# Half the sines of the even phases, wider evacuations, reordered cross sums, and two product differences made by negation and accumulating DMAs

## The chip, the cores and the metric

The kernel runs on one core of a Trainium2 chip, as one launch. The metric is the device time of the launch in microseconds (us), lower is better. The core has five engines that run side by side and wait for one another by semaphores: TensorE (PE, matmuls, with PEld for its weight loads), VectorE (DVE), ScalarE (ACT), GpSimd (POOL) and SyncE (SP, which only issues DMAs here). POOL issues the accumulating DMAs, which add a tile in SBUF to another one.

## The reference

Two branches over a sequence of 2048 positions and 640 channels, mixed by a gate for each position:

```python
def _A_ref(q, k, v, shift_k, ssm_k, ssm_D):
    k_shift = sum over t of k_pad[:, t:t + S, :] * shift_k[:, ks - 1 - t]   # ks = 4
    kv = k_shift * v
    y_f = rfft(kv padded to 2S) * rfft(ssm_k padded to 2S)                  # along the sequence
    y = irfft(y_f)[:S].astype(bfloat16)
    y = y + kv * ssm_D
    return q * y

def _B_ref(x, w1, b1, w2, b2):
    h = layernorm(x)                                    # over the 640 channels
    u = gelu(einsum("bsd,sf->bdf", h, w1) + b1)         # F = 1536
    y = einsum("bdf,fs->bds", u, w2) + b2
    return y.transpose(0, 2, 1)

g = sigmoid((q * gate_w).sum(-1, keepdims=True))
out = g * _A_ref(q, ...) + (1 - g) * _B_ref(q, ...)
```

The first branch is a long causal convolution for each channel, the second an MLP over the sequence dimension.

## The kernel before

The MLP is two streams of 384 matmuls of 128x128 by 128x320: `m1` (`pp<-X,ring`, weights from w1, followed by a gelu on ScalarE) and `m2` (`pp<-GT,W`, weights from w2). The convolution is done as a transform by matrices of sines (`FTB`, [128, phase 4, kt 2, cos/sin 2, k2 2, 128]), with the sequence split into four phases p and two halves h. The filter's transform (`wT` to `C[0]`, `C[1]`) and the signal's (`kv` to `C[2]`, `C[3]`) are matmuls on TensorE, evacuated from PSUM by ScalarE, and then mixed by VectorE with additions of 128x2560 (`mixing`, `mixing_acc`). Pointwise complex products follow (`cross`, `product`), then the inverse mixing (`invmix`) and the inverse transform (`inverse`, `pp<-C,FTB` and `pp<-SS,FTB`), whose evacuations are scaled by the gate, multiplied by q and added to the MLP's result `O1`.

What sets the order. The kernel doesn't write its instructions in the order of the code. Each operation is handed to a list planner (`_Sched`) with a duration, a priority and its dependencies. `run` plays the engines forward and picks, for each, the ready operation of lowest priority number; `emit` then writes the instructions in that order, and a tracker adds the semaphore waits. So the order on each engine is fixed at build time by the planner's own durations, and on the chip an engine waits in that order whatever else is ready. `after` edges force an order without a wait. In `run` a DMA gets an end: for every queue the transfer follows the DMAs before it at 365 GB/s, plus 2 us, and plus 6 us more if POOL issues it.

What the change and the prediction's steps touch:

- The head. `zz` spins (`SPIN`, line 798, and `WSPIN`, line 980) are matmuls on zeros put ahead of the filter's transposes and of the first transform. For each phase VectorE computes integer angles (`pint`), ScalarE takes a sine of 1024 elements. `transp` (line 862) transposes the filter through TensorE, `fwd_c` (line 878) transforms it in 16 groups of 4 matmuls of 320 columns, each evacuated by one ACTIVATE of 128x640.
- `k_turn` (line 760): a VectorE copy `kp<-kn` and a DMA transpose `KT<-kp` on SP. The first two turns stand between the layer norm statistics and their application. The third and fourth copies wait for two further k loads, which stand on SP behind the first two transposes.
- `kv` (line 1066): the short convolution, `pp<-KF,KT`, which needs both transposes of its half; its product `vkv<-ksh,vkv` or `kv<-ksh,v` is on VectorE.
- `mixing_acc` (line 1104): for each of two slots i, VectorE writes R(i) - R(2+i) to another place, and then a POOL DMA adds R(2+i) to R(i). Sums that read R(0) and R(1), written `C<-C`, wait for both DMAs.
- `product` (line 1201) with `into`: one product goes by an accumulating DMA into another tile, the real part is a 5120-wide product into `tm` and a subtraction.
- `acc_dma` (line 1222): two accumulating DMAs that add one of the products to another; they feed the second `invmix`.
- `inverse` (line 1275): TensorE needs the outputs of `invmix` from VectorE, phase by phase.
- W (w2) is loaded by SP, in pieces that wait until TensorE has finished with the part of `ring` that they overwrite.

The W loads and the accumulating DMAs share the core's DMA engines.

Of the kernel before, what the change touches and what calls it, by code (L numbers as in the profile page):

```python
# [9 lines left out]
BF16 = mybir.dt.bfloat16  # L10
# [3 lines left out]
ACT = mybir.ActivationFunctionType  # L14
# [314 lines left out]
class _Sched:  # L329
# [59 lines left out]
    def run(self):  # L389
# [14 lines left out]
        port = {"DVE": 0.0, "POOL": 0.0}  # L404
        dma_free = 0.3
        avail = {}
        for op in ops:
# [7 lines left out]
        t = 0.0  # L415
# [4 lines left out]
        while started < n:  # L420
# [6 lines left out]
            for e in engs:  # L427
# [31 lines left out]
                if e in ("SP", "QA") or op.lat < 0:  # L459
                    issue = 1.2 if e == "POOL" else 0.1  # L460
                    s = max(t + issue, dma_free)
                    dma_free = s + op.dur
                    op.end = dma_free + 2.0 + (6.0 if e == "POOL" else 0.0)
                    free[e] = t + issue
                else:
                    op.end = t + op.dur
                    if op.lock:
                        op.end += max(port["POOL" if e == "DVE" else "DVE"] - t, 0.0)
                        port[e] = op.end
                    free[e] = op.end  # L470
# [44 lines left out]
def _build(nc, A_q, A_k, A_v, A_shift_k, A_ssm_k, A_ssm_D, B_x, B_w1, B_b1, B_w2, B_b2, gate_w, out):  # L515
# [10 lines left out]
    with ExitStack() as es:  # L526
# [27 lines left out]
        def base_of(h):  # L554
            return T.mem[h.name][1]
# [56 lines left out]
        q_hi = alloc("q_hi", [128, 2, 4, D], BF16, at=base_of(Drow))  # L612
        assert base_of(KF) == base_of(Drow) + 1280
        cgb = [alloc(f"cgb{i}", [128, 2, D], BF16, at=base_of(GTB) + 2560 * i) for i in range(3)]

# [181 lines left out]
        memset("DVE", zz[:, :], 0.0, prio=-1)  # L797
        SPIN = (7, 3, 3, 2, 2)

# [9 lines left out]
        iota(acol[:, :], [[0, 1]], 0, 8)  # L809
        jr = lambda p, kt: iota(jrow[:, 2 * p + kt, :], [[-512 * (4 * kt + p), 2], [4 * (4 * kt + p), 128]], 4096 + 4 * kt + p, 0)  # L810
        for p in PORD:
            for kt in range(2):
                jr(p, kt).dur = 0.34
            if p == PORD[0]:
                iota(dif[:, :], [[1, 128]], 0, -1)
        iota(dif2[:, :], [[1, 32]], 128, -1)
# [6 lines left out]
        sins = {}  # L823
        for p in PORD:
            pv = V(pint, 1024 * p, [[512, 2], [256, 2], [1, 256]])
            t_ = tt("DVE", pv, V(tb, 0, [[0, 2], [256, 2], [1, 256]]), V(jrow, 512 * p, [[256, 2], [0, 2], [1, 256]]), ALU.add)
            if p != 0:
                t_.after.add(pprev)
            pa = pint[:, p, :, :, :].rearrange("q a b c -> q (a b c)")
            pprev = ts("DVE", pa, pa, 4095, None, ALU.bitwise_and, mode=4)  # L830
            if p == 0:
                ts("DVE", ident[:, :], dif[:, :], 0.0, None, ALU.is_equal)
            sins[p] = act(FTB[:, p, :, :, :, :].rearrange("q a b c d -> q (a b c d)"), pa, ACT.Sin, bias=cst[:, 0:1],
                scale=-(2.0 * math.pi / 4096.0) * (1.0 - 1e-6), name="sin")
        SC.add("DVE", 0.6, lambda s: T.op("DVE", lambda e: e.tensor_copy(ro, ri), [ri], [ro]), [ri], [ro], prio=0, name="taps")
# [26 lines left out]
        def transp(h, db):  # L862
            vt = _VT("cv")
            items = []
            for kt in range(2):
                for p in range(4):
                    o = (lambda s, j=4 * kt + p: s[:, 128 * j:128 * j + 128])
                    dfold = h == 0 and kt == 0 and p == 0
                    if dfold:
                        items.append((o, ident[0:1, :], Drow[0:1, 128 * db:128 * db + 128], True, False))  # L870
                    items.append((o, V(ssm, db * S + 1024 * h + 4 * kt + p, [[8, 128]]), ident[:, :], not dfold, True))
            m_ = mms(vt, (spin(SPIN[db]) if h == 0 else []) + items, name="wtr")
            m_.dur = (0.65 + 0.31 * SPIN[db] if h == 0 else 0.55)
            o_ = act(V(wT, 2 * h * SL + 128 * db, [[SL, 2], [D, 4], [1, 128]]), (lambda s: s[:, :].rearrange("q (a b c) -> q a b c", a=2, b=4)), ACT.Copy, vt=vt, name="wT")
            if h == 0:
                o_.after.add(sins[0 if db == 0 else 2])

        def fwd_c(p, ci, dst, scale):
            for k2 in range(2):
                vt = _VT("cv")  # L880
                items = []
                for kt in range(2):
                    for c in range(2):
                        items.append((chk(c), FTB[:, p, kt, c, k2, :], srcW(0)(kt, p, ci), kt == 0, kt == 1))
                m_ = mms(vt, (spin(WSPIN) if (p, ci, k2) == (PORD[0], 0, 0) else []) + items, name="W")
                m_.dur = 0.54
                act(V(dst, p * SL + k2 * D + 320 * ci, [[2 * D, 2], [1, 320]]), two, ACT.Copy, vt=vt, name="We", scale=scale)

# [59 lines left out]
        def ln_tile(hk, p):  # L948
# [6 lines left out]
            if t == 0:  # L955
                ops[0].after.add(pprev)
            o, i = mv[:, t, :], stats[:, t, :]
            ops.append(SC.add("DVE", 0.12, (lambda o, i: lambda s: T.op("DVE", lambda e: e.bn_aggr(o, i), [i], [o]))(o, i), [i], [o]))
# [20 lines left out]
        KFP = (0, 5, 10, 15)  # L979
        WSPIN = 3  # L980
        srcW = lambda h: (lambda kt, p, ci: wT[:, 2 * h + kt, p, 320 * ci:320 * ci + 320])
        for h in range(2):
            for db in range(ND):
                transp(h, db)
            if h == 0:
                consts()
            if h in (1,):
                fwd_even(srcW(h), h, C[h], 1.0 / 1024.0, h == 1, "W")
# [6 lines left out]
            if h == 0:  # L995
# [11 lines left out]

                pag = []

                def flush():  # L1010
# [5 lines left out]
                def stats_of(k):  # L1016
                    for t in range(LB[k], LB[k + 1]):
# [5 lines left out]
                        seq.append(b1)  # L1023
                        pag.append(ag)
                    ln_scale(LB[k], LB[k + 1])
                stats_of(0)
# [9 lines left out]
                for hk in range(2):  # L1036
                    k_turn(hk)
                mixing(C[0], SS, 0, fine=True, prio=MIXP)
            else:
# [161 lines left out]
        def product(dst, a, v, late=None, into=None):  # L1201
            if into is not None:
                tt("DVE", late, H(a, 1), H(v, 0), ALU.mult)
                dma(H(into, 1), late, 128 * 5120, stream="POOL", prio=0, accum=True)
                tt("DVE", P2(T0), P2(a), P2(v), ALU.mult)
                tt("DVE", H(dst, 1), H(a, 0), H(v, 1), ALU.mult)
                tt("DVE", H(dst, 0), H(T0, 0), H(T0, 1), ALU.subtract)
                return
# [116 lines left out]
        chained(product, A1[1], A1[1], V0[1], tmp_of(q_hi, 0), V1[1])  # L1325
        chained(product, A1[0], A1[0], V0[0], tmp_of(q_hi, 1), V1[0])
        acc_dma(A1[1], V1[1])
        acc_dma(A1[0], V1[0])
        chained(product, A0[1], A0[1], V0[1], H(V0[1], 0))
        lastacc = SC.ops[-1]  # L1330
        assert lastacc.eng == "POOL"
        for kt in range(2):
# [46 lines left out]
```

## Time and profile before

| | us |
|---|---|
| median of 3 runs | 180.29 (179.93 to 180.88) |
| the profiled execution | 179.5 |
| its span, first to last instruction | 177.7 |
| TensorE busy | 172.6 |
| VectorE busy | 169.7 |
| ScalarE busy | 117.0 |

The granted TensorE clock is 1.000 over the whole span. The difference between the profiled execution's time and its span, 1.8 us, lies outside the program's instructions. In the page each digit of a slice stands for a tenth of 4.4 us; a line of the order of time gives the start, the busy time, engine, source line, operation and tiles (buffer numbers left out), and in brackets an idle time before it and what ended it. For a DMA the trace also has the time from issue to landing. All matmuls have line L298 and all two-operand VectorE operations L632, so they are told apart by their tiles.

### The profile page before, as it was taken

The numbers are of one execution on the slowest core, as the hardware profiler recorded it, in microseconds if no ns is written. First come the engines' busy times: TensorE is split into PE (matmuls) and PEld (weight loads), VectorE is DVE, ScalarE is ACT, GpSimd is POOL, SyncE is SP. The second block draws the span as 40 slices with busy tenths as digits, with TensorE's granted clock in tenths as the row PEclk, the third lists the DMA queues.
The fourth block names the chain that finished last, engine by engine and source line by source line (L and its number), as shares of the span: only waits on it lengthen the run. The fifth ranks groups of instructions, "written<-read, shape, count | busy, mean of one in ns | idle before, by whom it ended". The sixth has DMA issues, their size and how long they took to land.

```text
span 177.7 us, 3342 instructions
## 1 busy us (share of the span) xinstructions
PE 172.6 (97%) x1380; PEld 129.4 (73%) x1381; DVE 169.7 (96%) x203; ACT 117.0 (66%) x176; POOL 43.6 (25%) x52
## 2 busy tenths in 40 slices
PE   7999999799999999999999999999999999999993
PEld 2666787487788776777777778888888887777772
DVE  7899789989999999999999999999999999999974
ACT  4999997998999999529999911231321323754760
POOL 8089803300000065000241101204343000252000
PEclk9999999999999999999999999999999999999999
DMA  4999999999999999999999998898999999499363
GB/s 136 394 411 374 391 312 156 248 414 374 191 240 315 109 216 226 231 228 278 230 227 271 205 248 299 144 225 230 188 193 217 207 218 408 167 197 212 93 241 131
DMA packets 38542, 43.51 MB, mean 245 GB/s; under 512 B 15867, under 2 KB 31360, under 8 KB 38528
## 3 DMA queue, kind: packets, MB, share of 16 engines
q1 hardware_dynamic: 33296, 32.16, 61.2%
q0 software_dynamic: 5200, 11.14, 36.5%
q8 instruction: 11, 0.18, 0.5%
q14 instruction: 3, 0.02, 0.0%
q10 hardware_dynamic: 32, 0.01, 0.0%
HBM read 25.87 MB, written 2.62 MB: 160 GB/s over the span
## 4 chain that ended last, share of the span: by engine, by line
PE 88%; DMA 5%; ACT 3%; SPq 2%; issue 0%; DVE 0%
PE pp L298 88%; DMA rows<-in_B_b_dram 5%; SPq L272 2%; ACT C L676 1%; ACT L676 1%; ACT GT L676 0%; DVE O L688 0%
## 5 line engine op out<-in xcount | busy, mean ns | idle before, releaser
L298 PE MATMUL pp<-X,ring 128*128 128x320 bf16 x384 | 55.3, 299 | 0.0
L632 DVE TENSOR_TENSOR C<-C 128x2560 bf16<-128x2560 bf16 (+2 forms) x37 | 54.5, 1523 | 0.8 <-ACT C L676 0.6
L298 PE MATMUL pp<-GT,W 128*128 128x320 bf16 x384 | 52.6, 299 | 0.0
L298 PEld LDWEIGHTS pp<-GT,W 128*128 128x128 bf16 x384 | 43.5, 113 | 8.7
L298 PEld LDWEIGHTS pp<-X,ring 128*128 128x128 bf16 x384 | 37.3, 98 | 14.3
L676 ACT ACTIVATE C<-pp 128x640 bf16<-128x640 f32 x64 | 40.7, 731 | 2.8 <-PE pp L298 2.7
L676 ACT ACTIVATE O<-pp,c,omg 128x640 bf16<-128x640 f32 x15 | 13.3, 885 | 34.7 <-PE pp L298 34.7
L267 POOL DMA_DIRECT2D C<-C x8 | 11.0, 1616 | 43.9 <-DVE C L632 43.9
L298 PE MATMUL pp<-wT,FTB 128*128 128x320 bf16 x112 | 17.1, 299 | 0.7 <-ACT GT L676 0.5
L676 ACT ACTIVATE cgb<-pp,gg 128x640 bf16<-128x640 f32 x16 | 12.7, 795 | 5.6 <-PE pp L298 5.2
L676 ACT ACTIVATE GT<-pp,cc 128x640 bf16<-128x640 f32 x12 | 9.6, 803 | 9.3 <-PE pp L298 9.2
L298 PEld LDWEIGHTS pp<-wT,FTB 128*128 128x128 bf16 x112 | 10.5, 98 | 5.6 <-ACT GT L676 0.8
L632 DVE TENSOR_TENSOR tm<-C,C 128x2560 bf16<-128x2560 bf16 (+1 forms) x7 | 14.3, 2059 | 0.0
L954 DVE BATCH_NORM_STATS2 stats<-X 128x6 f32<-128x320 bf16 x32 | 13.6, 464 | 0.5 <-DMA X<-in_A_q_dram 0.5
L298 PE MATMUL pp<-C,FTB 128*128 128x320 bf16 x96 | 13.4, 299 | 0.0
L267 POOL DMA_DIRECT2D C<-q_hi x6 | 5.9, 977 | 27.6 <-DVE C L632 12.9
L298 PEld LDWEIGHTS pp<-C,FTB 128*128 128x128 bf16 x96 | 9.4, 98 | 3.6
L676 ACT ACTIVATE gq<-gq 128x640 bf16<-128x640 bf16 x16 | 11.8, 745 | 0.2 <-DVE gq L632 0.2
L632 DVE TENSOR_TENSOR SS<-C 128x2560 bf16<-128x2560 bf16 x8 | 11.7, 1488 | 0.1
L632 DVE TENSOR_TENSOR C<-tm 128x2560 bf16<-128x2560 bf16 (+1 forms) x9 | 10.7, 1194 | 0.1
L676 ACT ACTIVATE ksh<-pp 128x1024 bf16<-128x1024 f32 (+1 forms) x12 | 9.9, 903 | 0.2 <-PE pp L298 0.2
L267 POOL DMA_DIRECT2D O<-q_hi x4 | 4.8, 1200 | 21.3 <-DVE q_hi L632 21.3
(77 smaller groups left out, 197.0 us busy)
## 6 DMA issues: line engine op xcount, KB each, us to landing
ring<-in_B_w_dram SPq DMA_DIRECT2D x12, 512.0 KB, 12.2
W<-in_B_w_dram SPq DMA_DIRECT2D x12, 512.0 KB, 5.5
C<-C POOLq DMA_DIRECT2D x8, 640.0 KB, 11.5
X<-in_A_q_dram SPq DMA_DIRECT2D x4, 640.0 KB, 8.4
kn<-in_A_k_dram SPq DMA_DIRECT2D x4, 640.0 KB, 9.4
out_dram<-O SPq DMA_DIRECT2D x7, 320.0 KB, 3.4
C<-SS POOLq DMA_DIRECT2D x3, 640.0 KB, 11.9
ssm<-in_A_ssm_k_dram SPq DMA_DIRECT2D x3, 512.0 KB, 6.8
```

The costliest lines, as they stand in the source:

```text
L267: ins = engobj.dma_start(out_ap, in_ap, accum_op=ALU.add, max_dma_last_dim=2560)
L272: ins = engobj.dma_start(out_ap, in_ap)
L298: ins = self.nc.tensor.matmul(ps_ap, lhsT=lhsT, rhs=rhs, start=start, stop=stop, skip_group_check=True)
L632: o_ = SC.add(eng, d, lambda s: T.op(eng, lambda e: e.tensor_tensor(o, a, b, op), rd, [o]), rd, [o], prio=prio, name="tt")
L676: return T.op("ACT", lambda e: e.activation(o, src, func, **kw), rr + [src], ww)
L954: ops.append(SC.add("DVE", 0.38, (lambda o, i: lambda s: T.op("DVE", lambda e: e.bn_stats(o, i), [i], [o]))(o, i), [i], [o]))
```

## The change

1. Sines. One ScalarE sine gives half of phases 0 and 2 (four blocks of 128 for each); phases 1 and 3 are as before. The other half of phases 0 and 2 is written by four VectorE multiplications with +1 or -1 out of the first half. The iotas that make the angles are cut to match.
2. Spins: 7, 1, 1, 1, 1 instead of 7, 3, 3, 2, 2, and none instead of 3 before the first transform.
3. Evacuations in `fwd_c`: 8 groups of 384 columns by two (768 evacuated at once), and 4 groups of 256 by four (1024 at once).
4. A small gelu right after the second half's transposes, which brings the table load with it.
5. The first two `k_turn` copies are put behind the statistics of tiles 13 and 15.
6. The planner's model of POOL DMAs: they follow each other at 2.2 times their transfer time, 1.8 us after issue at the earliest, beside the other queues.
7. `product` with `into`: the 5120-wide product and the subtraction become two products of 2560; the one to be subtracted is negated by ScalarE and added by an accumulating DMA.
8. The four DMAs of the two `acc_dma` calls are put behind the accumulate of the third product.

By items 6 and 7 the planner also moves operations that are not in the diff. On VectorE the two subtractions of `mixing_acc` for the last transform now stand together, and the two `C<-C` sums that read its DMAs stand eight product steps and the gate's sum after them, ahead of most of the products of `cross`. On TensorE the first inverse transform stands after 296 matmuls of `m2` (320 before), with 8 and 40 between and after its parts (40 before), and 40 at the end (24 before).

```diff
+        acc_free = 0.0
...
-                    s = max(t + issue, dma_free)
-                    dma_free = s + op.dur
-                    op.end = dma_free + 2.0 + (6.0 if e == "POOL" else 0.0)
+                    if e == "POOL":
+                        acc_free = max(t + issue + 0.6, acc_free) + 2.2 * op.dur
+                        op.end = acc_free
+                    else:
+                        s = max(t + issue, dma_free)
+                        dma_free = s + op.dur
+                        op.end = dma_free + 2.0
...
-        SPIN = (7, 3, 3, 2, 2)
+        SPIN = (7, 1, 1, 1, 1)
...
+            so = V(FTB, 0, [[2048, 2], [256, 4], [1, 128]]) if n_ == 0 else V(FTB, 1024 * (1, 3)[n_ - 1], [[1, 1024]])
+            si = V(pint, 0, [[512, 2], [128, 4], [1, 128]]) if n_ == 0 else pa
+            sins[(0, 1, 3)[n_]] = act(so, si, ACT.Sin, bias=cst[:, 0:1], scale=-(2.0 * math.pi / 4096.0) * (1.0 - 1e-6), name="sin")
+        for o_, i_, sg in (((640, 256), (512, 256), -1.0), ((128, 256), (0, 256), 1.0), ((2432, 256), (2048, 768), -1.0), ((2176, 768), (2304, 256), 1.0)):
+            h_ = ts("DVE", V(FTB, o_[0], [[o_[1], 2], [1, 128]]), V(FTB, i_[0], [[i_[1], 2], [1, 128]]), sg, None, ALU.mult, mode=4)
...
         def fwd_c(p, ci, dst, scale):
+            if ci == 1:
+                vt = _VT("cv")
+                items = []
+                for k2 in range(2):
+                    for c in range(2):
+                        for kt in range(2):
+                            items.append(((lambda s, j=2 * c + k2: s[:, 256 * j:256 * j + 256]), FTB[:, p, kt, c, k2, :], wT[:, kt, p, 384:640], kt == 0, kt == 1))
+                m_ = mms(vt, items, name="W")
+                act(V(dst, p * SL + 384, [[D, 4], [1, 256]]), lambda s: s[:, :].rearrange("p (a f) -> p a f", a=4), ACT.Copy, vt=vt, name="We", scale=scale)
+                return
...
-        WSPIN = 3
+        WSPIN = 0
...
+                g_ = act(gws[:, :], cst[:, 1:2], ACT.Gelu_apprx_tanh, name="tab", prio=SC.ops[-1].idx)
+                g_.after.add(SC.ops[-2])
...
                     k_turn(hk)
+                    SC.ops[-2].after.add(kpos[hk])
...
             if into is not None:
                 tt("DVE", late, H(a, 1), H(v, 0), ALU.mult)
                 dma(H(into, 1), late, 128 * 5120, stream="POOL", prio=0, accum=True)
-                tt("DVE", P2(T0), P2(a), P2(v), ALU.mult)
+                tn = (V(ngb, 0, [[1280, 2], [1, 1280]]), H(T1, 1))[npr[0]]
+                npr[0] += 1
+                tt("DVE", tn, H(a, 1), H(v, 1), ALU.mult)
+                act(tn, tn, ACT.Copy, scale=-1.0, prio=0, name="neg")
+                dma(H(into, 0), tn, 128 * 5120, stream="POOL", prio=0, accum=True)
                 tt("DVE", H(dst, 1), H(a, 0), H(v, 1), ALU.mult)
-                tt("DVE", H(dst, 0), H(T0, 0), H(T0, 1), ALU.subtract)
+                tt("DVE", H(dst, 0), H(a, 0), H(v, 0), ALU.mult)
                 return
...
+        n_acc = len(SC.ops)
         acc_dma(A1[1], V1[1])
         acc_dma(A1[0], V1[0])
         chained(product, A0[1], A0[1], V0[1], H(V0[1], 0))
         lastacc = SC.ops[-1]
+        for o_ in SC.ops[n_acc:]:
+            if o_.eng == "POOL" and o_ is not lastacc:
+                o_.after.add(lastacc)
```

## The prediction

> **What bounds the kernel now.** I read the page's busy sums and slices first, then the chain of work that ended last, then TensorE and VectorE in order of time, then the landing of single DMAs.
>
> The page's busy sums and slices, and two pieces of the chain:
>
> ```profile
> PE 172.6 (97%) x1380; PEld 129.4 (73%) x1381; DVE 169.7 (96%) x203; ACT 117.0 (66%) x176; POOL 43.6 (25%) x52
> ...
> PE   7999999799999999999999999999999999999993
> ...
> DVE  7899789989999999999999999999999999999974
> ...
> DMA  4999999999999999999999998898999999499363
> ```
>
> ```profile
> 35.02 139.97 PE pp L298 x1128
> 174.99 0.03 issue
> 175.02 0.55 DVE O L688
> ```
>
> TensorE runs without a gap from 35.02 to 174.99 us: it is the bound. But VectorE is at 96% too, and the DMA engines are full in nearly every slice. TensorE stays fed only because the second MLP product (`m2`, 384 matmuls) can be put before the inverse transforms, which need VectorE's results. So I look at where the two meet, in VectorE's and TensorE's order of time:
>
> ```profile
> 140.87 8.50 DVE L632 TENSOR_TENSOR C<-C 128x2560 bf16<-128x2560 bf16 x6
> ```
>
> ```profile
> 148.73 8.86 PE L298 MATMUL pp<-C,FTB 128*128 128x320 bf16 x64
> ```
>
> The fifth of these six sums is the first input of the inverse; at 1.42 us each it ends at 140.87 + 7.1 = 147.97. TensorE arrives at 148.73. VectorE is ahead by 0.76 us only, after 320 `m2` matmuls.
>
> Two places upstream fix when VectorE gets there. First, the copy that waits for the third k load, and an early wait for ScalarE (VectorE in order of time):
>
> ```profile
> 36.10 3.63 DVE L632 TENSOR_TENSOR C<-C 128x1280 bf16<-128x1280 bf16 x3 [0.65 <-ACT C L676]
> 39.94 0.83 DVE L764 COPY kp<-kn 128x2560 bf16<-128x2560 bf16 x1 [0.21 <-DMA kn<-in_A_k_dram]
> ```
>
> Second, the accumulating DMAs of `mixing_acc`, issued by POOL, and the sums that read their result:
>
> ```profile
> L267 POOL DMA_DIRECT2D C<-C x1: 1200/1200/1200, 84.9 to 84.9; - x1
> ...
> DMA to landing us min/median/max: 7.2/7.2/7.2
> ```
>
> ```profile
> L267 POOL DMA_DIRECT2D C<-C x1: 1200/1200/1200, 88.8 to 88.8; - x1
> ...
> DMA to landing us min/median/max: 10.7/10.7/10.7
> ```
>
> ```profile
> L272 SPq DMA_DIRECT2D W<-in_B_w_dram x3: 368/385/814, 85.9 to 88.1; - x3
> ...
> DMA to landing us min/median/max: 7.2/7.9/10.9
> ```
>
> ```profile
> 83.11 1.49 DVE L632 TENSOR_TENSOR C<-C 128x2560 bf16<-128x2560 bf16 x1
> ...
> 86.79 1.49 DVE L632 TENSOR_TENSOR C<-C 128x2560 bf16<-128x2560 bf16 x1
> ...
> 101.19 2.89 DVE L632 TENSOR_TENSOR C<-C 128x2560 bf16<-128x2560 bf16 x2
> ```
>
> The producers run at 83.11 and 86.79; the DMAs land at 84.9 + 7.2 = 92.1 and 88.83 + 10.7 = 99.6, because four W loads share the engines; the consumer comes at 101.19, 1.6 us after. The reader should see that this margin is small and that VectorE shows no gap there.
>
> **What the Trainium skill says.** "DMA: Bandwidth & Descriptors", section "Issuing engines are not separate DMA queues": DMAs of SP and POOL run on the same 16 engines and interleave. The trace agrees: an accumulate of 640 KB takes 5.8 us to land at 122.2, in quieter traffic, and 10.7 beside the W loads. "TensorE: Matmul & The Clock Gate", section "What's actually happening": TensorE's clock halves after an idle window of some 3.4 us. The trace fits at the start only: seven warm-up matmuls of 512 columns take 3.17 us, three later ones 0.81. "ScalarE activation tables: per-element evaluation and per-set limits", section "What a function is on this engine", puts two functions of different sets one table load, 1283 ns, apart; the trace has 1.28 us.
>
> **The change, part by part.**
>
> Head (half sines, wider evacuations, fewer spins, table load). One of four sines goes (1.06 us from start to start on ScalarE). Twelve evacuations replace sixteen: 640 columns cost 0.585 us apart and 1024 cost 0.905 (rows at 13 to 27 us), so 768 is worked out at 0.692; 8 x 0.692 + 4 x 0.905 = 9.16 against 9.36. Four small VectorE products (some 0.15 each, estimated from the 128x256 row at 0.30 in a slower mode) replace a pair of 0.69 + 0.42; both sit before X lands, where VectorE idles 0.5, so nothing. Nine of twenty spin matmuls go: 9 x 0.21 = 1.9 us of TensorE, but they only filled waits. The table load (1.28) moves from 31.60, before the first gelu that TensorE waits for, into ScalarE's 0.88 us idle at 27.8. Before 35.02 TensorE shows 1.2 us of waits behind these. TensorE then reaches the conv product `kv` 1 to 2 us earlier, where KT lands at 33.9 as now (the moved k turn costs nothing: the first still starts at about 22.7, when kn lands, and the second transpose is issued at 27.95 behind the first). After the second KT landing (51.1) I keep a gain of 1.25 us for TensorE; bounds 0 and 2.2.
>
> VectorE gains 1.3 to 2 us up to 37.7, and loses it all: the copy of the third k tile waits for kn at 39.9, and that load is queued on SP behind the two transposes, which do not move. From there to the 80s the changed order holds the same VectorE operations, so it is where it was: gain 0.
>
> Products. Each of the two on A1 loses one 5120-wide product (2.87) and two or three 2560-wide steps change places: 14.63 us for both from 110.40 to 125.03 becomes 4 x 1.45 x 2 = 11.6, so VectorE saves 3.0. ScalarE gets two negations of 2560 (0.72 for the 640-wide bf16 row, and 1920 more elements at the 0.32 us that lie between 640 and 1024: 2.3 us each), in idle gaps of 2.4 between O evacuations. POOL gets two more 640 KB accumulates.
>
> Reordering. TensorE's order now has 296 `m2` matmuls before the inverse instead of 320, so it wants its first input 24 x 0.1358 = 3.26 us earlier, plus its head gain: at 148.73 - 3.26 - 1.25 = 144.2. VectorE without a new wait delivers at 147.97 - 3.0 = 144.9. That alone would be level.
>
> New wait. The planner used to put an accumulate at 11 us or more (8 us beyond its transfer); it now takes 2.2 times the transfer plus 1.8, 5.75 us for 640 KB and 3.95 more for the next one. In the new order both `mixing_acc` subtractions stand together (83.1 and 84.5) and the sums that read the results come after six small products and two of 2560, at 83.1 + 2.8 + 9.05 = 94.95. The second DMA is issued at 86.3 instead of 88.8, but it follows the first in its queue, and the first is issued at 84.9 as now. Total work on the DMA engines is the same: from 86 to 98.5 they carry two accumulates and three W loads (W at 1.4 us each leaves 4.1 for each accumulate). I put the landing at 98.5: VectorE waits 98.5 - 94.95 = 3.5 us with every later product queued behind it, and, over VectorE's gate sum, ScalarE's tanh and the evacuations after it; those are first missed at about 107, so that part is hidden. Bounds: landing at 92.1 + 3.4 = 95.5 (3.4 is the spacing of two accumulates landing at 128.1 and 131.5), a wait of 0.5; or at 99.6 as now, a wait of 4.6. I take 3.5, since the engines have no free time in these slices.
>
> Sum. First inverse input at 144.9 + 3.5 = 148.4; TensorE waits 148.4 - 144.2 = 4.2 us, having gained 1.25. End moves by -1.25 + 4.2 = +2.9 us. The TensorE gain cancels: the shift is the wait less 0.6. What follows keeps its distance (40 instead of 24 matmuls are left at the end, which TensorE must do anyway; one 320 KB store now goes out on SP between the last two of 160 KB, issued before the last matmul group ends, 0 to 0.3 us, taken as 0). Against the profiled execution's 179.5 us (span 177.7) that is 182.4; the median of the three runs is 0.8 higher, so 183.2.
>
> **Rivals.**
>
> Landing in time, no change: the second accumulate lands near 95.5 to 96; wait 0.5 to 1.5, shift -0.1 to +0.9, 180.2 to 181.2. For it: the DMA is issued 2.5 us sooner. Against: it stands behind the first and three W loads.
>
> Faster: the landing is before 95 and VectorE keeps some of its head gain (the kn load lands earlier than 39.9); then TensorE's 1.25 counts: about 179.1. For it: TensorE's busy share and 1.2 us of removed waits. Against: the pin at 39.94.
>
> Much slower: the nine accumulates in a row (seven now, with 3.4 to 5 us between landings from 128.1 to 149.1) start at about 115 and, with W and q loads beside them, end at 157 or later, while the second inverse mixing wants the last one at about 156; each us beyond that, less 0.7 of slack, is paid. An idle of 4.2 us can also halve TensorE's clock for a stretch (up to 1.7 us more). Together 185 to 187.
>
> **Chances and range.** Wait of 2 to 4.6 us (181.7 to 184.3): 0.58. Much slower: 0.14. No change: 0.13. Faster: 0.15. A measurement of this kernel can tell 0.5%, 0.9 us, from nothing. So faster 0.15, same 0.13, slower 0.72. The range 179.7 to 185.6 leaves out most of the faster case and the upper half of the much slower one; the likeliest case alone has 181.7 to 184.3.
>
> **What would show it.** In the changed profile: a VectorE idle of 2 to 4.6 us near 95 put down to a DMA of C<-C, at the sum that in the kernel before starts at 101.19; TensorE idle of about 4 us at 144, before pp<-C,FTB; kp<-kn still at 39.9 with some 2 us idle before it; `kv` from about 34; the POOL accumulates from 115 landing one after another until about 155. If VectorE runs through the 90s without a gap, the forecast is wrong, and the time is below 180.3. If the gap is there and TensorE has none at 144, VectorE's savings were larger than 3 us.

## The result and the profile after

The changed kernel takes 187.32 us (median of 4 runs, 186.45 to 187.8) against 180.45 us (179.93 to 180.88) for the kernel before on the same chip: a ratio of 1.0377, 95% interval 1.0326 to 1.0427. The forecast was 183.2 with a range up to 185.6: slower was right, the size was not. The profiled execution has a span of 185.4 us against 177.7.

In three of the runs further down one execution is left out of the times: with the planner's model alone the profiled one, which was disturbed (span 362.8 us, so no time of its trace is used); with the k loads first one of 627.92 us; and with the sums later the profiled one, the slowest of four (186.54 us), whose trace is shown all the same.

The page of the changed kernel, busy sums and slices (one digit for each of 40 slices):

```profile
PE 173.9 (94%) x1371; PEld 130.4 (70%) x1372; DVE 166.5 (90%) x205; ACT 120.2 (65%) x174; POOL 44.8 (24%) x54
...
PE   7799999999999999999999999999999349999994
...
DVE  7599997989999999999958999999949997998573
...
PEclk9969999999999999999999999999999957999999
```

VectorE's busy share fell from 96% to 90%, and it has two holes, near slices 21 and 30. TensorE has one hole, at 145 to 151 us, and its granted clock drops right behind it. The two holes of VectorE, in its order of time (start, duration, what; in brackets the idle time before and who ended it):

```profile
95.44 0.18 DVE L638 TENSOR_TENSOR gth<-sd,gacc 128x16 f32<-128x16 f32 x1 [0.56 <-ACT gq L682]
98.24 1.49 DVE L638 TENSOR_TENSOR C<-C 128x2560 bf16<-128x2560 bf16 x1 [2.62 <-DMA C<-C]
...
138.01 2.83 DVE L638 TENSOR_TENSOR tm<-C,C 128x5120 bf16<-128x5120 bf16 x1 [2.43 <-DMA C<-tm]
140.87 2.89 DVE L638 TENSOR_TENSOR C<-tm 128x2560 bf16<-128x2560 bf16 x2
143.68 8.50 DVE L638 TENSOR_TENSOR C<-C 128x2560 bf16<-128x2560 bf16 x6
```

The first hole is the one that was forecast: `mixing_acc`'s first sum stands where its accumulate has not landed. The second was not: the last product writes a `tm` buffer while the accumulating DMA of the second negation still reads it. The chain of waits runs through both:

```profile
86.54 11.61 DMA C<-C
...
123.63 14.29 DMA C<-tm
138.01 2.84 DVE tm L638
140.87 9.92 DVE C L638 x7
150.79 0.14 issue
150.92 31.77 PE pp L298 x216
```

The transfer from `tm` is issued at 123.63 and takes 14.29 us to land. Two 640 KB accumulates stand ahead of it in POOL's queue: the one from `ngb`, issued at 119.18, lands at 130.5, and the one from `q_hi`, issued at 122.66, at 133.8. The first inverse input is the fifth of the six sums from 143.68 and ends at 150.8. TensorE in order of time, and by stage (length, then busy time of PE, PEld, DVE, ACT and POOL, the granted clock, the DMA share, GB/s):

```profile
139.74 5.73 PE L298 MATMUL pp<-GT,W 128*128 128x320 bf16 x41
150.92 8.94 PE L298 MATMUL pp<-C,FTB 128*128 128x320 bf16 x48 [5.45 <-DVE C L638]
```

```profile
145.00:150.00 5.00, 0.47 (x4) 0.13 (x2) 5.00 (x5) 0.31 (x1) 0.00 (x0) 0.87 1.05 269
150.00:155.00 5.00, 4.08 (x16) 2.31 (x17) 4.96 (x4) 0.79 (x1) 0.00 (x0) 0.50 1.08 259
155.00:160.00 5.00, 5.00 (x37) 3.53 (x36) 3.78 (x5) 3.27 (x5) 1.52 (x2) 0.94 0.89 224
```

TensorE stops for 5.45 us and then works at half its clock: 18 matmuls from 150.92 on follow each other at about 0.261 us instead of 0.1358, which is 2.26 us lost. These two numbers make up the whole difference at TensorE's end: TensorE's last matmul ends at 182.68 instead of 174.98, 7.70 us later, and 5.45 + 2.26 = 7.71. Its `m2` matmuls before the inverse end at 145.47; 24 matmuls of 0.1358 earlier than 148.73 is 145.47 too, so in this execution the head had brought TensorE nothing by then.

### The profile page after: what moved, and what is told of

Same layout as the page of the kernel before. It is cut to its first block, busy times and chain, and to the rows that moved or that the text cites. A ratio compares the mean times of both kernels' runs of the same rounds, so it can differ in the third digit from the quotient of the medians.

```text
span 185.4 us, 3331 instructions
## 1 busy us (share of the span) xinstructions
PE 173.9 (94%) x1371; PEld 130.4 (70%) x1372; DVE 166.5 (90%) x205; ACT 120.2 (65%) x174; POOL 44.8 (24%) x54
## 3 DMA queue, kind: packets, MB, share of 16 engines
HBM read 25.87 MB, written 2.62 MB: 154 GB/s over the span
## 4 chain that ended last, share of the span: by engine, by line
DVE 35%; PE 34%; DMA 17%; ACT 9%; issue 2%; POOL 1%; SPq 0%; DVEq 0%
PE pp L298 34%; DVE C L638 24%; DMA C<-tm 8%; DMA C<-C 6%; ACT C L682 5%; DVE tm L638 4%; DMA ssm<-in_A_ssm_k_dram 3%; DVE q_hi L638 3%; ACT ksh L682 2%; DVE kv L638 2%; ACT wT L682 2%; DVE gq L638 1%; POOL C L267 1%; DVE ngb L638 1%; ACT GT L682 0%
## 5 line engine op out<-in xcount | busy, mean ns | idle before, releaser
L682 ACT ACTIVATE C<-pp 128x640 bf16<-128x640 f32 (+2 forms) x60 | 39.8, 765 | 3.6 <-PE pp L298 3.6
L267 POOL DMA_DIRECT2D C<-C x8 | 10.5, 1491 | 46.5 <-DVE C L638 43.0
L298 PE MATMUL pp<-C,FTB 128*128 128x320 bf16 x96 | 15.8, 330 | 5.5 <-DVE C L638 5.5
L298 PEld LDWEIGHTS pp<-C,FTB 128*128 128x128 bf16 x96 | 10.2, 107 | 10.7 <-issue 5.7
L298 PE MATMUL pp<-wT,FTB 128*128 128x320 bf16 (+2 forms) x112 | 16.5, 299 | 0.0
L638 DVE TENSOR_TENSOR tm<-C,C 128x2560 bf16<-128x2560 bf16 (+1 forms) x7 | 13.1, 1871 | 2.5 <-DMA C<-tm 2.4
L682 ACT ACTIVATE wT<-pp 128x1024 bf16<-128x1024 f32 x10 | 9.9, 1118 | 1.7 <-PE pp L298 1.6
```

The source lines that it names most:

```text
L267: ins = engobj.dma_start(out_ap, in_ap, accum_op=ALU.add, max_dma_last_dim=2560)
L298: ins = self.nc.tensor.matmul(ps_ap, lhsT=lhsT, rhs=rhs, start=start, stop=stop, skip_group_check=True)
L638: o_ = SC.add(eng, d, lambda s: T.op(eng, lambda e: e.tensor_tensor(o, a, b, op), rd, [o]), rd, [o], prio=prio, name="tt")
L682: return T.op("ACT", lambda e: e.activation(o, src, func, **kw), rr + [src], ww)
```

## The experiments

The theory after the result: the planner's new order (sums ahead of their transfer, 24 fewer matmuls ahead of the inverse) and the `tm` buffer make VectorE late, TensorE idles for it, and its clock falls. The rivals: the new operations cost it by themselves; the head loses it (spins, clock); TensorE's idle is harmless because VectorE's last sums decide anyway. Ratios are to the kernel before on the same chip, with 95% intervals.

| run | ratio | interval |
|---|---|---|
| head alone | 1.0046 | 1.0029 to 1.0064 |
| tail alone | 1.0555 | 1.0514 to 1.0597 |
| changed, planner's model as before | 1.0165 | 1.0108 to 1.0222 |
| changed, spins put back | 1.0392 | 1.0342 to 1.0442 |
| changed, one negation | 1.0133 | 1.0084 to 1.0183 |
| changed, 336 matmuls ahead of the inverse | 1.0248 | 1.0213 to 1.0282 |
| changed, TensorE kept busy in the idle | 1.0313 | 1.0257 to 1.0369 |
| changed, sums later | 1.0270 | 1.0216 to 1.0324 |
| changed, sums later and one negation | 1.0016 | 1.0004 to 1.0028 |
| head alone, 24 matmuls held for the end | 0.9988 | 0.9974 to 1.0002 |
| the same, k loads first | 0.9998 | 0.9982 to 1.0014 |
| planner's model alone | 1.0541 | 1.0511 to 1.0570 |
| planner's model and reordered accumulates | 1.0365 | 1.0323 to 1.0408 |
| the same, sums later | 1.0179 | 1.0120 to 1.0238 |
| harmless parts together | 1.0029 | 1.0013 to 1.0046 |

**Head alone, tail alone.** The first has all edits of the head and none of the planner, products and accumulates; the second the reverse.

```diff
-        SPIN = (7, 3, 3, 2, 2)
+        SPIN = (7, 1, 1, 1, 1)
...
-                    op.end = dma_free + 2.0 + (6.0 if e == "POOL" else 0.0)
+                    if e == "POOL":
+                        acc_free = max(t + issue + 0.6, acc_free) + 2.2 * op.dur
...
+                act(tn, tn, ACT.Copy, scale=-1.0, prio=0, name="neg")
```

(the first hunk stands for the head, the others for the tail)

> The kernel before with the head of the change alone (half sines, wider evacuations, fewer spins, table load, the tied k turn); products, order of the sums and the planner's model of POOL's transfers as before. Theory A (the loss is made by the tail, and the head's gain on TensorE is eaten by its slower start): 180.4, within 0.9 us of before. Theory B (the forecast's gain of 1.25 us for TensorE is real and is only hidden in the changed kernel by the idle at 145): 179.2, and TensorE then has VectorE's margin of 0.76 us against it. Theory C (the head itself loses, by a halved clock between 5 and 15 us): 181.5 or more.

> The kernel before with the tail of the change alone (two negations with accumulating DMAs, reordered accumulates, new planner model of POOL's transfers); the head as before. Theory A (the tail makes all of the loss): 187, with waits of VectorE near 95 (C<-C, 2.6 us) and near 138 (tm, 2.4 us) and TensorE idle for some 5 us before the first inverse matmul. Theory C (the head adds a us or more to it): 185 to 186.

The head alone took 180.69 us against 179.96, the tail alone 189.48, more than the whole change. With the head alone TensorE's first inverse matmul starts at 148.27 instead of 148.73, 0.46 earlier with the same 320 matmuls ahead of it. Two waits in the middle took the rest; the list of waits of that run (total, times, longest):

```profile
PE pp L298 <- DVE vkv L632: 0.4, 1, 0.4
...
PE pp L298 <- DMA KT<-kp: 0.4, 1, 0.4
```

Neither is in the kernel before. And the end got longer: this planner left 12 `m2` matmuls behind the last inverse instead of 24, TensorE ends at 174.52, and VectorE's last sums come after that:

```profile
175.43 1.01 DVE L688 SCALAR_TENSOR_TENSOR O<-pp,omg,cgb 128x320 bf16<-128x320 f32 x2
```

So the head alone costs 0.8 us (0.0046 x 180), near Theory A; Theory C's clock is not the reason, as it was 1.00 between 5 and 15 us (0.88 and 0.78 in the two halves of this stretch in the changed kernel's own profile). In the tail alone VectorE waits 4.90 us at the sum instead of 2.62: without the changed head the second accumulate is issued at 89.11 instead of 86.54 and lands at 100.12 instead of 98.15. It idles TensorE 6.67 us. The head, worth nothing alone, takes 2.3 us of this wait off by moving that issue.

**The planner's model undone in the changed kernel.**

```diff
-                    if e == "POOL":
-                        acc_free = max(t + issue + 0.6, acc_free) + 2.2 * op.dur
...
+                    op.end = dma_free + 2.0 + (6.0 if e == "POOL" else 0.0)
```

> The changed kernel with one thing undone: the planner books an accumulating DMA as before (8 us beyond its transfer, in the common queue). All new operations stay. Theory of the order (the new operations cost little, the plan that expects them early costs the time: 296 m2 matmuls before the inverse in place of 320, and sums put before their DMA has landed): 180 to 182, no TensorE idle over 1 us at 145, no wait near 95. Rival (the negations and their DMAs cost it by themselves, through the wait of 2.4 us for the tm buffer and nine accumulates in a row): 184 or more, with the wait near 138 still there and TensorE idle after it.

182.58 us, above the theory's band and below the rival's. Its waits:

```profile
DVE SS L633 <- DMA C<-C: 3.7, 1, 3.7
...
DVE q_hi L633 <- DMA q_hi<-in_A_q_dram: 2.2, 1, 2.2
...
PE pp L298 <- DVE C L633: 1.7, 1, 1.7
```

The waits near 95 and 138 and TensorE's idle at 145 are gone, as the theory has it, with 320 `m2` matmuls ahead of the inverse again. The wait near 138 is gone although the second negation still goes through `tm`: this plan issues its accumulate first of three, and it lands 6.8 us later, at 127.2, before the buffer is needed. POOL in order of time, in the changed kernel and here:

```profile
119.18 1.20 POOL L267 DMA_DIRECT2D C<-ngb  x1 [2.58 <-ACT ngb L682]
122.66 1.20 POOL L267 DMA_DIRECT2D C<-q_hi  x1 [2.29 <-DVE q_hi L638]
123.63 1.47 POOL L267 DMA_DIRECT2D C<-tm  x1
```

```profile
120.41 1.20 POOL L267 DMA_DIRECT2D C<-tm  x1 [7.03 <-ACT tm L677]
121.15 1.70 POOL L267 DMA_DIRECT2D C<-ngb  x1
121.87 2.20 POOL L267 DMA_DIRECT2D C<-q_hi  x1
```

But the negations are not free: with them POOL's accumulates finish too late for the second inverse mixing, the place that a rival of the forecast named. More than half of the loss is the order's; the 3.0 us that are left (0.0165 x 180) belong to operations and head.

**Spins put back in the changed kernel** (`SPIN` 7,3,3,2,2 and `WSPIN` 3).

> The changed kernel with the nine removed spin matmuls put back (7,3,3,2,2 and 3). Theory C (fewer spins let TensorE's clock fall between 5 and 15 us, and the head's gain goes with it): TensorE reaches the inverse a us earlier, but it waits there for VectorE, so the time stays at 187.3 within 0.5; the granted clock between 5 and 15 is back near 1. Rival (spins only filled waits; the clock fell because the ssm loads landed a us later): the clock between 5 and 15 stays below 0.9.

187.21 us, unchanged. The clock between 5 and 15 is 1.00 here, but it is 1.00 with few spins too (head alone, and the changed head with the old planner), so few spins do not lower it by themselves. In the changed kernel's own profile the second `ssm` load landed at 7.12 us instead of 5.75, and TensorE waited 1.3 us for it. Whether the clock fell for that is open: with the head alone and 24 matmuls held (further down) TensorE waits 1.23 us for a later `ssm` load, with few spins, and the clock stays at 1.00. As the time is unchanged, the spins are cleared of the loss.

**One negation fewer.**

```diff
+                if npr[0] == 2:
+                    tt("DVE", P2(T0), P2(a), P2(v), ALU.mult)
+                    tt("DVE", H(dst, 1), H(a, 0), H(v, 1), ALU.mult)
+                    tt("DVE", H(dst, 0), H(T0, 0), H(T0, 1), ALU.subtract)
+                    return
```

> The changed kernel with the second product as in the kernel before (no negation, one accumulate fewer; VectorE has 1.4 us more of work). Theory (the step left out of the forecast: the first tm product of the last product waits 2.4 us for the negated accumulate that reads tm): no VectorE wait for DMA C<-tm, first inverse input at 150.8 - 2.4 + 1.4 = 149.8, TensorE, with 312 m2 matmuls before it, idles about 2.1 us and its clock stays at 1.0 after it: 182 to 183. Rival (the tm wait only stood in for another late transfer, such as the accumulates before it in POOL's queue): a wait of about the same size for another DMA, and 185.5 or more.

182.13 us. VectorE, with more to do, is earlier:

```profile
DVE C L638 <- DMA C<-C: 2.2, 1, 2.2
PE pp L298 <- DVE C L638: 2.0, 3, 1.6
```

There is no wait for C<-tm, and none of its size has taken its place. TensorE's first inverse wait is 1.56 us, and its clock is 1.00 after it. The whole kernel is about 4.4 us faster without the second negation ((1.0377 - 1.0133) x 180), though it has 1.4 us more of VectorE's work. Not all of that is the `tm` wait: in this plan 312 `m2` matmuls stand ahead of the inverse, 16 more than in the changed kernel, so TensorE also comes to it later (146.90 instead of 145.47), which is 1.4 us less to wait.

**TensorE's order by hand.**

```diff
-                    mms(vt, items, name="inv")
+                    m_ = mms(vt, items, name="inv")
+                    m_.after.add(m2s[(41, 46)[h]])
```

> The changed kernel with TensorE's order alone set by hand: 336 m2 matmuls before the first inverse in place of 296, and 48 after its 64. VectorE has the same waits, so its input comes at 150.8 as before. Theory 1 (TensorE's idle of 5.5 us and the halved clock behind it are most of the loss): no idle over 0.5 us, clock 1.0 at 150 to 155, 182 to 183.5, the rest being VectorE's own lateness of 3 to 4 us in the second inverse mixing. Theory 2 (VectorE's lateness alone decides, since the last inverse and the last sums wait for it): 185.5 or more.

184.29 us, between the two. The clock stays at 1.00 in the profiled execution (in the other three, which were a little shorter, the mean clock was 0.991 to 0.993, so it fell somewhere in them), but 2.20 us of idle are left: VectorE waited 3.4 us at the `tm` product (2.43 before; the profile names an evacuation of `O` by ScalarE, which the product does not read and which ended within 0.2 us of the landing of the accumulate from `tm`), and TensorE now starts with a tile that the sixth of VectorE's sums writes, not the fifth, so its first matmul is at 153.17. TensorE's idle and clock are worth some 2.3 us here; the rest goes with VectorE's lateness, which this order of TensorE does not hide.

**TensorE kept busy in the idle.**

```diff
+                    warm = [((lambda s: s[:, 0:512]), V(FTB, 0, [[1, 128]]), GT[:, 0, 0:512], True, True)] * (24 if (h, p, kt) == (0, 2, 0) else 0)
+                    m_ = mms(vt, warm + items, name="inv")
```

> The changed kernel with 24 idle matmuls of 512 columns put before the first inverse matmul, where TensorE waits 5.5 us. They compute nothing that is kept. Theory (the halved clock between 150 and 157 costs 2.1 us of the end): clock 1.0 at 150 to 155, 185.2. Rival (VectorE's later sums would hide a faster TensorE there): 187 within 0.5.

```profile
144.91 5.34 PE L298 MATMUL pp<-GT,FTB 128*128 128x512 bf16 x24
150.44 6.69 PE L298 MATMUL pp<-C,FTB 128*128 128x320 bf16 x48 [0.19 <-DVE C L638]
```

185.14 us. In its order of time 48 inverse matmuls take 6.69 us, where the changed kernel needs 8.94: 2.25 us, the halved clock. Its last matmul ends 2.72 us earlier, 0.48 of it because its inverse starts at 150.44. The medians differ by 1.2 us only (0.0064 x 180), with intervals that overlap, so the size rests on the traces.

**The sums later.**

```diff
+                if n_ == 2:
+                    for a_ in accsum:
+                        a_.after.add(SC.ops[-2])
```

(`accsum` holds the two sums in `mixing_acc`, `n_` counts the cross products)

> The changed kernel with the two sums that read mixing_acc's accumulated results tied behind one more cross product (2.5 us of VectorE's work), so that they start where the second accumulate has landed. Theory (the two waits on transfers add): no wait of VectorE near 95, every later product 2.6 us earlier, first inverse input at 148.2, TensorE idles 2.8 us, clock not halved: 182.5 to 183.5. Rival (the negated accumulates are bound by the DMA engines, not by their issue, so the tm wait grows by what the first wait loses): wait at tm of 4 to 5 us, 186.5 to 187.5.

185.26 us, 2 us above the theory's band, which had the clock stay. The wait near 95 is gone, the one for `tm` grew from 2.43 to 2.98, and the inverse starts at 149.03, 1.9 us earlier, with the same 296 matmuls ahead of it: the waits mostly add, and the rival has a small part. The clock still fell, after an idle of 3.51 us (the mean clock of this execution is 0.981, that of the other three 0.990 to 0.991):

```profile
149.03 9.62 PE L298 MATMUL pp<-C,FTB 128*128 128x320 bf16 x48 [3.51 <-DVE C L638]
```

**Both waits away.** The last edit and the single negation together.

> The changed kernel with both new waits of VectorE taken away: the sums of mixing_acc tied one cross product later, and the second product as in the kernel before. Theory (the two waits and what TensorE makes of them are the whole loss): VectorE without a gap over 0.6 us between 90 and 145, first inverse input at about 146.5, TensorE idle under 0.5 us before it: 180 to 181. Rival (nine accumulates in a row end too late for the second inverse mixing, so what VectorE wins it waits for there): a VectorE gap of 2 us or more at SS<-C near 154, 181.5 to 182.5.

```profile
DVE SS L638 <- DMA C<-C: 0.7, 1, 0.7
...
PE pp L298 <- DVE C L638: 0.6, 2, 0.5
DVE gth L638 <- ACT gq L682: 0.6, 1, 0.6
...
DVE C L638 <- DMA C<-C: 0.2, 1, 0.2
```

180.04 us against 179.76: all but 0.3 us of the loss is gone, with the planner's model, the reordering, the head and one negation still in. TensorE does not idle before the first inverse matmul, at 147.36. The rival's wait is there with 0.7 us and costs little. This is the run that shows the cause: the two waits of VectorE and what TensorE makes of them. It does not part the waits from TensorE's order, as the planner again puts 312 matmuls ahead of the inverse; with 296 TensorE would have come some 2.2 us earlier (16 x 0.1358, an estimate) and idled for up to that long.

**Looking for a gain.** The head with 24 matmuls held behind the last inverse, and that with SP's k loads ahead of its v loads:

```diff
+                    if h == 1 and p == 3:
+                        m2s[-2].after.add(m_)
...
-        for hk in range(2):
-            v_load(hk)
         for hk in range(2, 4):
             k_load(hk)
+        for hk in range(2):
+            v_load(hk)
```

> The head alone (as the first run) with TensorE's last 24 m2 matmuls kept behind the last inverse, where the head alone left 12. Theory (the head gains 0.46 us of TensorE, and lost it because VectorE's last sums then ended 1.4 us after TensorE): TensorE ends at 174.5 as there, VectorE's last sum right after it, 179.4, that is 0.5 below before. Rival (the C inputs of the second inverse are late for the earlier start): TensorE idles there and the time is 180.5 or more.

> The run with the head and 24 held m2 matmuls, and the third and fourth k loads put ahead of the first two v loads on SP. Theory (VectorE is pinned by the k load landing at 39.9, as the forecast said; TensorE's waits at 48 and 51 come from it): the k load lands near 37, both waits go, 178.6. Rival (the v load, now later, pins vkv and VectorE instead): no gain, 179.4 or more.

The first took 179.53 us (22 runs) against 179.76: the 1.0 us that the head alone lost at its end is back, and the forecast 0.5 below before is at most half there. In the second the k load is used at 35.98 instead of 40, and the time stays at 179.71. VectorE was pinned by that load, but unpinning it is worth nothing that the times show: behind 40 us TensorE then has four waits of 0.20 to 0.31 us elsewhere, the last before the inverse at 148.35.

**The planner's model alone, and with the reordered accumulates.** The kernel before with the new model of POOL's transfers; then with the tie of the change that puts the four accumulates on A1 behind the one that q_hi's loads wait for.

```diff
+            if o_.eng == "POOL" and o_ is not lastacc:
+                o_.after.add(lastacc)
```

> The kernel before with the planner's new model of POOL's transfers alone: the same operations in another order (mixing_acc's sums earlier on VectorE, 328 m2 matmuls before the inverse in place of 320). Theory (the plan alone makes a wait): VectorE waits 4 to 5 us for C<-C near 95, nothing is saved in the products, TensorE idles some 3 us at 150, 182.5 to 185. Rival (the plan harms only together with the new accumulates): within 0.9 us of before.

> The kernel before with the planner's new model and the reordered accumulates of the change, but with head and products as before. Theory (the order that the plan makes costs the time, through the one wait of mixing_acc's sums, since without negations there is no tm wait): VectorE waits 4 to 5 us for C<-C near 95 as in the run with the tail alone, first inverse input near 152.5, TensorE, with 312 m2 matmuls before it, idles about 5 us and its clock halves: 186 to 188. Rival (the plan alone was slow only because it put four accumulates ahead of the one that q_hi's loads wait for, which the reordering mends): 180 to 182.

189.59 us with the model alone, 9.7 us above before (0.0541 x 180) and far above the theory's band. In its order the accumulate that the q_hi loads wait for stands behind four others; how much of the 9.7 us that is was not seen in a trace. With the tie it is 186.81 us, as much as the whole change costs, with no new operation and none removed:

```profile
PE pp L298 <- DVE C L637: 4.8, 1, 4.8
...
DVE C L637 <- DMA C<-C: 4.8, 1, 4.8
```

Tying those four costs 3.2 us less than leaving them in front ((1.0541 - 1.0365) x 180), which is the rival's point, but the loss that is left is not the rival's 180 to 182. It has the theory's numbers: VectorE waits 4.8 us for the accumulate, TensorE 4.8 us for VectorE, and the clock halves behind it. Of the two waits only the first is there, longer than in the changed kernel (4.8 us instead of 2.62). Then the same with the sums one cross product later:

> The same with mixing_acc's sums tied one cross product later. Theory: the wait near 95 shrinks by 2 us or more, and the time with it by at least that and the halved clock, to 180 to 183. Rival (the wait is not what the plan costs): no change from the run without the tie.

```profile
151.57 1.25 PE L298 MATMUL pp<-C,FTB 128*128 128x320 bf16 x8 [2.65 <-DVE C L637]
```

183.36 us, 3.45 less. VectorE's wait shrank by 2.3 us (4.80 to 2.48), TensorE's by 2.2; the rest is the clock, which stayed at 1.00. That is above the theory's 180 to 183 by a little: the tie by one product is too short here.

**The harmless parts together.** Both waits away, k loads first, 312 matmuls ahead of the inverse.

> The changed kernel with both new waits taken away (sums tied later, one negation), the k loads ahead of the v loads, and 312 m2 matmuls before the first inverse: the parts of the change that were not shown to cost, together. If TensorE's wait of 1.0 us for vkv at 48 goes and no other takes its place: TensorE ends near 174.4 and the time is 178.9 to 179.2, 0.4% below before. Rival (what TensorE gains in the head ends at VectorE's last sums): 179.7 or more.

180.57 us, as high as the rival has it, but not for the rival's reason: TensorE's wait for vkv at 48 went, and one of 1.17 us for ScalarE's copy of C came at 41.30, so TensorE reached the inverse no earlier (147.79, 147.36 with both waits away). No version measured here beats the kernel before by more than its measurement is uncertain.

## Why the prediction was wrong, step by step

- *TensorE gains 1.25 us in the head (bounds 0 and 2.2)*: at the inverse it is 0.46 with the head alone and 0.0 in the changed kernel's profile. Within the bounds, mis-sized. Up to `kv` it was right: that starts at 34.03 instead of 35.02 with the head alone, and between 33.3 and 34.2 in all the runs with the changed head. Only the changed kernel's own profile has 35.26, after its late `ssm` load. Behind `kv` the forecast named the KT landing at 51.1 and kept 1.25 beyond it; with the head alone, waits for vkv and KT at 48 to 51 took most of what was won.
- *VectorE is pinned by the k load at 39.9*: right. `kp<-kn` starts at 40.05. That the pin costs anything is not shown: the run with k first gained nothing.
- *Products save 3.0 us*: 2.91. The A1 products take 11.72 us, from 113.61 to 125.33.
- *The second accumulate lands at 98.5 and VectorE waits 3.5 us for it (0.5 to 4.6)*: right. It landed at 98.15, and VectorE waited 2.62, after 0.56 for ScalarE's `gq`, together 3.18. The products start 3.21 us later than before (113.61, 110.40).
- *First inverse input at 148.4*: it came at 150.8. **This is the step that failed.** The two negations and their accumulates were booked as ScalarE work in idle gaps and as 1.3 MB more in POOL's queue, and the forecast did not ask who needs the buffers they read. The second negated product sits in `tm`, and VectorE's last product is due to overwrite it at 135.6, 12 us after that accumulate is issued, while it takes 14.29 to land: 2.43 us of wait. With it, 148.4 + 2.4 = 150.8. Taking that negation out took the wait away and, with 16 more matmuls planned ahead of the inverse, 4.4 us of the time. The negation alone does not make the wait: under the planner's old model it stays, its accumulate goes first of three, and there is no wait. A run with another buffer for it was not made.
- *TensorE waits 4.2 us*: 5.45. It is 4.2 + 2.4 from the line above, less 1.2 for the gain that it did not have, so the gain cancels as the forecast said.
- *Shift = wait less 0.6*: this left out the clock, **the second failing term**. The forecast put a halved clock (up to 1.7 us) into a rival with 0.14, although its own idle of 4.2 us was above the 3.4 us that the Trainium skill ("TensorE: Matmul & The Clock Gate", section "What's actually happening") gives for the idle window, and which it cited. With such an idle it belonged to the likeliest case. It measured 2.26 us.
- *Nine accumulates in a row end at 157 or later*: the last landed at 157.77. In the changed kernel it delays nothing, since the second inverse mixing is late anyway; in the run with the old planner the same place waits 3.7 us.
- *The tail keeps its distance*: right. From TensorE's end to the span's end it is 2.7 us in both.

Forecast and missing terms add up: 2.9 + 2.4 (tm) + 2.3 (clock) = 7.6 us, against 7.7 in span. The rival *much slower, 185 to 187* came nearest, for half of its reason.

What stays open: how the 9.7 us of the planner's model alone divide, how the gain of both waits away divides between the waits and the 16 matmuls, and why the vkv wait appears in the middle of some runs with the head and not in the changed kernel's profile.

## What to carry to other kernels

When an operation is handed to an asynchronous transfer, price three things: its landing, whoever reads the result, and whoever next writes the buffer that it reads from; the last is the one that is easily missed. When an order is planned from a model of transfers, look at the sum or matmul that the plan moves ahead on the strength of it: here the new model and the reordered accumulates, without any new work, cost as much as the whole change. And an idle of the matmul engine is priced with the slow stretch behind it as soon as it reaches the length at which the clock falls.

## What the runs showed of the hardware

- In the profiled executions the clock of TensorE stayed at 1.00 after idles of 1.56, 2.20 and 2.65 us, and fell to half after 3.51, 4.83, 5.45, 5.83 and 6.67 us; this agrees with the 3.4 us of the page named above. One fall does not fit: in the changed kernel's profile the clock is at half from about 9 to 12 us, where the longest idle before it is 1.25 us. The slow stretch that followed the long idles differed more than I expected: 2.9 to 6.1 us, 1.4 to 2.9 us of it lost, and the longest came after the shortest of these idles. At the very start of the kernel before the profile's 1.00 does not fit the matmuls: the first seven of 512 columns take 3.17 us there, 0.45 us each, and three later ones 0.81, 0.27 us each. The two sides in the stretch from 150 to 155 us, first after 2.65 us of idle, then after 3.51:

```profile
150.00:155.00 5.00, 3.27 (x23) 2.20 (x24) 4.97 (x5) 1.53 (x2) 0.00 (x0) 1.00 1.08 264
```

```profile
150.00:155.00 5.00, 5.00 (x20) 2.79 (x19) 3.86 (x4) 1.59 (x2) 0.00 (x0) 0.50 1.07 203
```

- An accumulating DMA of 640 KB from one buffer of the core to another took 5.8 us from issue to landing in the kernel before (at 122.2) and up to 18.8 in the changed one (issued at 138.9), where those in a row landed 3.0 to 5.4 us apart. The one from `tm` took 6.8 us where it was issued first of three and 14.29 where it was issued last. With the size the same, what stands ahead in the queue decides much of the landing.
